# Moving the loads of two weight matrices and of half of x behind the first tile of y, and planning the modulation loads with later landings

## The chip, the core and the metric

One core of a Trainium2 chip. The metric is the device time of one execution in microseconds, lower is better. Times are read from a hardware profile of one execution and from repeated unprofiled executions of the same program.

## What is computed

All tensors are bf16. S = 2048 positions, D = 640 channels, F = 1728 hidden features.

```python
mod = silu(c) @ w_mod            # (640) @ (640, 6*640) -> sa, ca, ga, sb, cb, gb
h = layernorm(x) * (1 + ca) + sa
# A: a shift filter of 4 taps on k, times v, then a long causal convolution over S by FFT
kv = shift4(k, shift_k) * v
y  = irfft(rfft(kv, 4096) * rfft(ssm_k, 4096))[:S] + kv * ssm_D
x  = x + ga * (h * y)
h  = layernorm(x) * (1 + cb) + sb
# B: w1, gelu, shifts along S by +-1 and +-2 rows per quarter of the channels, w2; then w3, gelu, w4
h1 = h + shifts(gelu(layernorm(h) @ w1)) @ w2
out = x + gb * (h1 + gelu(layernorm(h1) @ w3) @ w4)
```

## The kernel before

The convolution is a two-level FFT made of matmuls. It works on channels in five blocks of 128 (`b`), then on positions in 16 tiles of 128 (`A` or `t`).

Stages, by their helper functions:

- `stage1` (L408) and `stage2` (L425): the forward transform of the filter s, block by block. `to_slots` (L395, a 32x32 transpose on DVE) brings each block into shape; `evac` (L208 on ACT, L210 on DVE) copies each PSUM result to SBUF.
- `k_shift` (L480, evacuated by a multiply with v, L485): the 4-tap shift. k and v come in transposed, one block at a time, by transposing DMAs on SP's queue (L234). Each multiplied block then goes through `to_slots`, `stage1` (L408) and `stage2_half` (L446).
- `inverse1` (L633 multiplies, L644 and L645 matmuls) and `inverse2` (L685): the inverse transform. `inverse2` leaves y for two or three tiles at a time in `Rb`, called `y_all`.
- `mod_half` (L503 load, L509 matmul, L516 to L524 evacuation): one half (320 columns) of one of the six modulation vectors. Twelve halves in the order ga, ca, sa (the first six; buffers in `RH` and `RK`, three in rotation) and then cb, sb, gb (the last six; buffers in `R3`).
- `x_load` (L540), `ln1_stats` and `ln1_fin` (L554 to L577), `make_q` (L610, L617, L618): the first layernorm and q.
- `chain_a`, `chain_b`, `chain_c`: for a tile, x += q*y with the sum for the next layernorm (L761, L764); a sum of squares on ACT (L753); the scale, made on POOL (L738 to L741); the second h (L775 or L779, then L780); its layernorm (L748 or L610). `turn` transposes the result by PE (L796) for the first tiles and by DMA on SP (L789) for the later ones.
- `mm_w1` (L842, L852), `mm_w2` (L897), `mm_w3` (L931), `mm_w4` (L961): the four matmul layers of B, in groups of one or two tiles. The result goes out from SP (L993).

Nothing is scheduled on the chip. Every piece of work is a task of the `Planner`, in a list with a number. A text, `ORDER`, gives the order in which all tasks are issued: a task number, a letter for its engine (P TensorE, A ScalarE, D VectorE, G GpSimd, S the SP queue), and, for matmuls, the PSUM buffers (0 to 3) that it uses. `run` only checks that a task's dependencies stand ahead of it in the list:

```python
            assert t.deps <= seen and len(places) == len(t.alloc)
```

The costs, the landing times (`lat`, `rate`) and the reads and writes (`r`, `w`) given to `add` served the search that produced the text. The waits on the chip come from the layer below, which finds which instructions touch the same memory. Each engine takes its own instructions in the order of the text.

In `ORDER` of before, SP has the last six modulation halves, one 40 KB piece of w2 among them, then x of tiles 8 to 15 in four transfers of 320 KB, mixed with w1 (800 KB), w2 (640 KB and four pieces of 40 KB) and the tail of w4. w3 and w4 take the place of what `inverse2` reads.

Of the kernel before, what the change touches and what calls it, by code (L numbers as in the profile page):

```python
# [15 lines left out]
S, D, F = 2048, 640, 1728  # L16
P = 128
# [9 lines left out]
18D 19G 20D 21G 23D 24A 22D 27G 29D 36G 37G 30A 28D 50G 0S 2S 68G 69D 25A 31A 26G 84P:0 86P:1 88P:2 51D 53A 4S 72G 73D 106P:3 85A 87A 38G 104P:0 89A  # L27
107A 6S 3S 70G 71D 39G 40A 102P:1 103A 5S 74G 98P:2 99A 105D 8S 90P:3 91A 49G 118P:0 75D 110P:1 9S 119D 94P:2 32G 111A 95A 112P:3 113A 108P:0 109A
116P:1 114P:2 115A 1S 66D 67D 96P:3 117D 80P:0 82P:1 10S 122P:2 41G 42G 43G 44A 97A 52D 54A 45D 81A 83D 11S 123D 33G 78P:3 79A 100P:1 101D 76P:0 77A
136D 92P:2 34S 47S 120P:3 121D 93A 179P:1 55G 180A 46S 7S 193P:0 194A 35S 195P:2 196A 181P:1 147P:0 148A 182D 201S 141P:3 142D 139P:2 140A 143P:1  # L30
199P:0 175P:3 200A 48S 176A 144D 204S 185P:2 186D 161P:1 162A 65G 157P:0 158D 171P:3 172A 203S 165P:2 166D 191P:1 192A 167P:0 155P:3 156A 168D 169P:2
170A 177P:1 178D 189P:0 190A 151P:3 159P:2 160A 202S 152D 145P:1 146D 187P:0 188A 149P:3 150D 197P:2 198A 183P:1 184D 153P:0 154A 163P:3 164A 262P:2
173P:1 174A 12S 137P:0 138A 13S 214D 263A 126P:3 56G 264P:1 210D 254D 127D 57G 124P:0 125D 211D 58G 59G 60A 61G 62G 63G 265A 260P:2 215A 266P:1 267A
261A 14S 255D 64A 15S 128P:3 129D 258P:0 259A 270P:1 271A 130P:2 131D 256D 16S 212A 276P:0 277A 268P:1 269A 132P:3 134P:2 17S 133D 135D 257D 282P:0
209A 283A 223S 213G 224P:1 225A 220S 278P:3 226S 286P:2 287D 279A 221P:0 222A 272P:1 273A 274P:3 275A 227P:0 228D 469D 284P:1 463D 342S 285A 292P:2
293D 288P:0 289A 232S 233P:3 234D 290P:1 291D 466D 296P:2 297A 294P:0 295A 229S 230P:3 231D 343G 310P:1 302P:2 303A 311D 235S 460D 312P:3 313A 298P:0
299D 308P:1 309A 236P:2 237D 467D 300P:3 301A 306P:0 307D 280P:2 281A 316P:1 317D 252G 314P:3 315A 253S 304P:0 305D 318P:2 319A 248G 247G 320P:1 321A
241S 336P:3 340P:2 341A 337A 243G 240S 330P:0 331A 338P:1 339A 367G 251S 250G 239S 326P:2 322P:3 323A 464D 345D 344D 348P:0 349A 244G 346P:1 347A 352D
245S 249G 334P:3 238S 242S 351G 246G 335A 350S 353D 356P:0 357A 354P:1 366S 324P:3 325A 327D 359G 332P:2 333A 358S 360D 361D 362P:0 363A 368D 364P:3
328P:2 329A 355A 369D 370P:0 371A 365A 376D 375G 374S 372P:2 377D 378P:1 379A 380P:0 373A 381A 384D 217A 382S 383G 385D 388P:3 389A 391G 390S 393D  # L40
392D 386P:1 400D 387A 396P:2 397A 394P:0 398S 399G 401D 402P:3 425S 403A 404P:1 405A 408D 395A 426P:2 407G 406S 409D 416D 410P:3 415G 414S 417D 412P:1
431S 411A 465D 413A 461D 462D 427D 216G 420P:0 421D 418P:3 419A 470D 422S 423P:1 424D 471D 468D 218A 475P:20 476A 477D 520D 499D 434S 456S 500D 521D
540D 541D 543D 459G 472A 435P:3 436A 523D 473D 474D 432P:1 437S 438P:2 219G 501A 433A 512A 478P:03 439A 522A 502G 503G 428S 429P:1 430A 504D 505D 542A
491P:21 525D 479A 524G 507D 526D 528D 492A 506A 480A 568D 527A 545D 485P:02 487A 493A 486A 206S 544G 546D 547A 207S 508G 509D 510P:3 529G 511A 530D
531P:2 532A 482P:10 481G 569D 570A 548D 452S 571D 572D 574D 573A 458G 517P:3 518A 205S 513D 536P:2 533D 484D 549G 483A 550D 534D 575G 580D 581D 576D
455S 582D 457S 577D 578D 208S 514D 538P:3 584D 537A 535D 634D 635D 631D 539A 583A 488P:01 551P:2 552A 579A 585G 586D 515P:3 589D 632D 449D 489A 558P:2
516A 637D 559A 556P:0 557A 636A 453S 587P:3 633A 638G 590P:2 591A 490A 497S 588D 454S 560P:0 561D 562A 643D 600P:2 601A 639D 494S 563G 564G 598P:3
599A 498G 640D 641D 565D 566P:1 602P:0 605P:2 642A 644D 645D 647D 646A 648G 441D 649D 650S 567A 618P:3 446A 616P:1 603D 604A 651D 652S 620P:0 553A
496S 619A 606D 661P:2 617A 443D 607A 440D 608G 609G 613D 659P:3 610D 622P:1 444D 621A 554D 555D 699D 700D 662A 660A 614P:0 615A 611P:2 666P:3 667D
663P:0 612A 683P:2 623A 442G 664D 701A 668A 684A 665A 669G 670G 671A 679P:1 680A 677P:3 495S 674D 672P:0 675P:2 678A 592D 593D 595D 596D 597D 673A  # L50
594D 702D 624P:1 676A 749P:3 765D 766D 703D 704A 681P:0 747P:2 750A 682A 445G 653D 654D 655D 768D 769D 770A 705G 706G 625D 626D 767A 745P:3 685P:10
748A 743P:2 771G 707D 708D 711D 709D 710A 686P 712D 713D 772G 773D 777A 715G 714A 716G 717A 718S 774D 778D 779D 780A 775D 776A 744A 781D 719D 720S
687D 746A 447D 782G 783A 785D 448G 729P:1 730A 786S 727P:2 728A 784S 795P:3 721A 656D 693D 796A 657D 658D 831D 628S 832D 793P:0 450D 694D 724A 451G
722D 734P:1 723D 794A 834D 835D 836A 697S 787D 735D 731P:2 732D 737D 797P:3 798D 833A 751P:01 696S 688D 837G 838G 843D 800P:2 736A 725D 752P 844D 845D
733A 738G 741D 689S 839A 840D 841D 739A 801D 803D 627S 799A 847D 802A 740S 842A 846A 742S 753D 811P:3 812A 804G 807D 805A 815P:2 788D 809P:0 848G 851D
816A 813P:3 810A 849D 726D 852S 850S 855P:2 856A 808S 790D 853P:0 806S 873P:2 759D 854A 860P:1 791D 792D 891D 892D 789D 951D 952D 954D 857P:0 894D
895D 629S 893A 814A 861D 897D 896A 630S 898G 899D 900D 858D 863D 692S 875P:3 876A 871P:1 869P:3 691S 872A 754D 757S 870A 695S 817P:01 901D 874A
877P:32 818P 862A 859A 864G 903D 819D 758S 904D 905D 906A 865D 867D 868S 866S 907D 902A 908G 909D 911D 953A 955G 956D 957D 935P:0 936A 958D 960G 959A
961G 878P 690S 760D 825D 756S 912S 755S 519G 962D 826D 885D 910S 915P:0 916A 913P:1 914A 698S 820D 879D 931P:0 762S 963S 966P:2 967A 964P:1 917P:3
918D 920P:2 921D 822S 965A 969P:1 970D 932A 968G 1003P:0 933P:3 929P:2 827S 828S 919A 922A 923G 924G 927D 928S 764S 925D 926S 1004D 1005A 972P:1 973D  # L60
934A 971A 930A 937P:03 987P:2 761S 988A 981P:1 983P:2 763S 880D 884S 883S 824S 823S 821S 886D 887S 890S 939D 975D 974A 976G 985P:0 977A 979D 889S 982A
829S 938P 945D 882S 984A 978S 986A 980S 1016P:1 1014P:2 1010P:0 1017A 1011A 881S 1015A 1012P:3 1006G 1007G 1008D 1009S 989P:10 1013A 946D 830S 940D
941S 991D 947S 1032P:2 888S 992D 993S 996S 943S 1038P:3 990P 997D 1036P:1 1033A 1042D 1037A 1018P:20 995S 949S 1034P:1 1035A 1019P 944S 942S 998D
1002S 1000S 999S 950S 1020D 948S 1021D 1023S 1025S 1026D 1039A 994S 1027D 1001S 1024S 1040P:21 1022S 1043D 1030S 1028S 1031S 1044D 1045D 1047S 1048S
1046S 1029S 1049S 1041P 1050D 1051D 1055A 1052S 1053A 1054S
# [72 lines left out]
def kernel(  # L138
# [63 lines left out]
    def dma(eng, kb, fn, r=(), w=(), rate=330.0):  # L202
        return add(eng, {"SP": 0.5, "POOL": 0.6}, lambda e: fn(nc.sync if e == "SP" else nc.gpsimd), r, w, kb=kb, rate=rate)
# [297 lines left out]
    def mod_half(i, j, hf):  # L501
        w, wk = wm[i % 3] if i < EARLY else wl[i - EARLY]
        dma("SP", 410, lambda q: q.dma_start(w, mod_d[:, :, j * D + 320 * hf:j * D + 320 * hf + 320]), w=[wk], rate=340.0)  # L503
# [34 lines left out]
    def x_load(a0, a1):  # L538
        for cg in range(4):
            dma("SP", 41 * (a1 - a0), lambda q, cg=cg: q.dma_start(x_all[32 * cg:32 * cg + 32, a0:a1, :], x_pos.rearrange("(a c) n d -> c n a d", c=4)[cg, :, a0:a1]),  # L540
                w=[("Ra", D * a0, D * a1, "x")], rate=275.0)
# [39 lines left out]
    x_load(8, NT)  # L581
# [77 lines left out]
    junk = RG[:, 7040:7680]  # L659
    ln1_all((8, 10), (10, 12), (12, 14), (14, 16))  # L660
    dma("SP", 800, lambda q: q.dma_start(w1_sb, B_w1.rearrange("(b p) n -> p b n", p=P)), w=[("RG", 0, 3200)])
    dma("SP", 700, lambda q: q.dma_start(w2_sb[:, 0:4, :], B_w2.rearrange("(g r) n -> r g n", g=4)[0:P]), w=[("RG", 3200, 6400, "w2")])
    for g in range(4):
        dma("SP", 60, lambda q, g=g: q.dma_start(w2_sb[32 * g:32 * g + 32, 4, :], B_w2[160 * g + P:160 * g + 160, :]), w=[("RG", 3200, 6400, "w2")])
    add("POOL", 0.8, lambda e: nc.gpsimd.tensor_copy(w1x.rearrange("p b (g r) -> p b g r", g=4), w1_sb.rearrange("p b (g r) -> p b g r", g=4)[:, :, :, P:160]),
# [423 lines left out]
```

## Time and profile before

| What | us |
| --- | --- |
| median of 3 runs | 303.29 (301.24 to 303.41) |
| the profiled execution, whole | 302.69 |
| its span in the profile | 301.0 |
| busy: PE, PEld, DVE, ACT, POOL | 271.0, 207.3, 220.8, 204.4, 108.9 |
| first matmul | 8.43 |
| first matmul of inverse2 | 98.20 |
| first y evacuated | 100.67 |
| PE at half clock (windows of 2 us that show 0.50) | 106 to 118, and 124 to 126 |
| PE without holes from | 143.13 |

The page's slices give, for each engine, the busy share of a fortieth of the span (7.5 us) in tenths; the windows give the same in us of 10. The chain is the work that ended last, followed back to what released each step; "issue" is time in which an engine waited for nothing that the profile shows. SP's rows are the issue of DMAs, not their transfer.

### The profile page before, as it was taken

How to read it: one execution, taken by the hardware profiler on the slowest of the kernel's cores; microseconds unless marked ns; L12 is line 12 of the kernel's file. 1: busy time of each engine (PE TensorE's matmuls, PEld its weight loads, DVE VectorE, ACT ScalarE, POOL GpSimd, SP SyncE). 2: the span in 40 equal slices, each digit the busy share in tenths (PEclk: the TensorE clock that was granted, in tenths of full speed). 3: DMA queues.
4: the chain of work that ended last, by engine and by line, in shares of the span. 5: the costliest groups of instructions: out<-in, count | busy, mean ns of one | idle time of the engine just before them, and what ended most of it. 6: DMA issues, size and time to landing. Idle time of an engine off the chain costs nothing.

```text
span 301.0 us, 7658 instructions
## 1 busy us (share of the span) xinstructions
PE 271.0 (90%) x3054; PEld 207.3 (69%) x3054; DVE 220.8 (73%) x446; ACT 204.4 (68%) x345; POOL 108.9 (36%) x238
## 2 busy tenths in 40 slices
PE   0899999979989576878999999999999999999993
PEld 0665655758888345756888787688867887887771
DVE  7999999979999979998659969983547343231343
ACT  4798999979999869998864679646451642604110
POOL 4967641451256646242345534310125120300000
PEclk9999999999999955799999999999999999999999
DMA  5998999998899940352900040234014112310121
GB/s 180 272 221 189 200 195 234 235 201 215 224 258 293 257 107 2 108 208 44 293 6 1 2 93 14 54 68 43 18 23 93 40 29 60 75 30 19 46 54 45
DMA packets 58179, 35.75 MB, mean 119 GB/s; under 512 B 39872, under 2 KB 54848, under 8 KB 58144
## 3 DMA queue, kind: packets, MB, share of 16 engines
q1 hardware_dynamic: 56944, 31.88, 45.2%
q0 software_dynamic: 1104, 3.34, 4.2%
q8 instruction: 24, 0.39, 0.5%
q14 instruction: 11, 0.09, 0.1%
q10 hardware_dynamic: 96, 0.04, 0.1%
HBM read 16.31 MB, written 2.62 MB: 63 GB/s over the span
## 4 chain that ended last, share of the span: by engine, by line
PE 71%; ACT 11%; DVE 6%; DMA 6%; issue 3%; POOL 1%; SPq 0%; ACTq 0%; DVEq 0%; POOLq 0%
PE ps_w L931 19%; PE ps_w L961 19%; PE ps_w L897 6%; PE ps_ksh L480 6%; PE ps_s L408 6%; PE ps_w L842 4%; ACT T L208 4%; ACT R L208 3%; PE ps_s L425 2%; PE ps_mod L509 2%; DMA RH<-in_w_mod_dram 2%; DMA Ra<-in_A_ssm_k_dram 2%; DVE R L780 1%; PE ps_i L644 1%; PE ps_s L446 1%
## 5 line engine op out<-in xcount | busy, mean ns | idle before, releaser
L931 PE MATMUL ps_w<-R,T 128*128 128x256 bf16 (+1 forms) x630 | 64.0, 261 | 0.0
L931 PEld LDWEIGHTS <-T 128*128 128x128 bf16 x630 | 55.7, 98 | 7.2 <-issue 1.1
L961 PE MATMUL ps_w<-T,R 128*128 128x320 bf16 x416 | 59.2, 299 | 0.0
L935 ACT ACTIVATE R<-ps_w 128x1024 bf16<-128x1024 f32 (+2 forms) x36 | 29.1, 828 | 42.1 <-PE ps_w L931 42.1
L961 PEld LDWEIGHTS <-R 128*128 128x128 bf16 x416 | 40.2, 98 | 15.8 <-ACT R L935 0.3
L208 ACT CAST T<-ps_s 128x1024 bf16<-128x1024 f32 x34 | 32.7, 1023 | 1.1 <-PE ps_s L408 1.1
L984 DVE TENSOR_TENSOR T<-ps_w,R 128x640 bf16<-128x640 f32 x15 | 12.3, 823 | 27.3 <-PE ps_w L961 14.0
L408 PE MATMUL ps_s<-F1bd,Rb 128*128 128x256 bf16 x160 | 22.9, 294 | 8.4 <-DVE Rb L395 8.4
L753 ACT ACTIVATE RG<-R 128x640 bf16<-128x640 bf16 x32 | 23.6, 736 | 10.2 <-DVE R L904 7.1
L208 ACT CAST R<-ps_s 128x640 bf16<-128x640 f32 (+1 forms) x36 | 26.7, 828 | 2.8 <-PE ps_s L446 1.9
L738 POOL TENSOR_TENSOR lnv<-stat,lnv 128x2 f32<-128x2 f32 x19 | 4.9, 256 | 62.6 <-ACT RG L753 33.0
L408 PEld LDWEIGHTS <-Rb 128*128 128x128 bf16 x160 | 16.4, 105 | 14.7 <-DVE Rb L395 8.8
L904 DVE SCALAR_TENSOR_TENSOR R<-ps_w,R 128x640 bf16<-128x640 f32 x16 | 13.1, 821 | 14.5 <-PE ps_w L897 14.5
L739 POOL TENSOR_TENSOR lnv<-lnv,mhalf 128x2 f32<-128x2 f32 (+1 forms) x29 | 22.3, 770 | 2.3
L897 PE MATMUL ps_w<-RG,R 128*128 128x320 bf16 x160 | 23.1, 299 | 0.0
L842 PE MATMUL ps_w<-R,RG 128*128 128x256 bf16 (+1 forms) x200 | 21.0, 267 | 0.3 <-ACT Rb L208 0.3
L644 PE MATMUL ps_i<-EA,Rb 128*128 128x128 bf16 x160 | 19.1, 219 | 1.2 <-ACT T L208 0.4
L645 PE MATMUL ps_i<-EB,Rb 128*128 128x128 bf16 x160 | 19.0, 219 | 0.5 <-DVE Rb L633 0.5
L897 PEld LDWEIGHTS <-R 128*128 128x128 bf16 x160 | 15.4, 98 | 6.0 <-issue 0.3
L842 PEld LDWEIGHTS <-RG 128*128 128x128 bf16 x200 | 18.2, 107 | 1.7 <-issue 0.4
L480 PE MATMUL ps_ksh<-R,RQ 128*128 128x512 bf16 x80 | 18.8, 380 | 0.0
L858 ACT ACTIVATE R<-ps_w1x 32x256 bf16<-32x256 f32 (+1 forms) x40 | 13.2, 330 | 7.8 <-PE ps_w1x L852 7.5
(179 smaller groups left out, 524.3 us busy)
## 6 DMA issues: line engine op xcount, KB each, us to landing
Ra<-in_A_ssm_k_dram SPq DMA_DIRECT2D x5, 512.0 KB, 5.6
Ra<-in_A_q_dram SPq DMA_DIRECT2D x8, 320.0 KB, 6.7
R<-in_w_mod_dram SPq DMA_DIRECT2D x6, 400.0 KB, 6.3
out_dram<-RH SPq DMA_DIRECT2D x60, 40.0 KB, 1.6
T<-in_B_w_dram SPq DMA_DIRECT2D x1, 2160.0 KB, 8.5
T<-in_B_w_dram SPq DMA_DIRECT2D x1, 2080.0 KB, 9.5
RH<-in_w_mod_dram SPq DMA_DIRECT2D x4, 400.0 KB, 4.3
RK<-R POOLq DMA_DIRECT2D x5, 256.0 KB, 4.5
```

The costliest lines, as they stand in the source:

```text
L208: nc.scalar.copy(dst, src(ps.tile))
L408: nc.tensor.matmul(psv[:, ml, :], lhsT=xL[:, s0:s0 + P], rhs=F1r, start=True, stop=True)
L480: nc.tensor.matmul(pt[:, i, :], lhsT=diagw[:, b, jj, :], rhs=kT[:, b, c0:c0 + 512], start=(jj == 0), stop=(jj == 3))
L644: nc.tensor.matmul(psv[:, w, :], lhsT=Av[:, r_, :, g_], rhs=EAf, start=True, stop=False)
L645: nc.tensor.matmul(psv[:, w, :], lhsT=Bv[:, r_, :, g_], rhs=EBf, start=False, stop=True)
L739: nc.gpsimd.tensor_tensor(rs, rs, mhalf[:, 0:n], ALU.pow)
L753: add("ACT", 0.74, lambda e: nc.scalar.activation(junk, src, ACT.Square, scale=float(D) ** -0.5, accum_out=stat[:, li, 1, t:t + 1]), r=[sk ...
L842: nc.tensor.matmul(pt[:, fb, 0:cw], lhsT=w1_sb[:, b, 160 * fb:160 * fb + P], rhs=hT[:, b, 0:cw], start=(b == 0), stop=(b == ND - 1))
L897: nc.tensor.matmul(pt[:, hf, 0:320], lhsT=gsf[:, fb, c0:c0 + P], rhs=w2_sb[:, fb, 320 * hf:320 * hf + 320], start=(fb == 0), stop=(fb == 4))
L931: nc.tensor.matmul(pt[:, fl, 0:cw], lhsT=w3_sb[:, b, fb * P:(fb + 1) * P], rhs=xT[:, b, 0:cw], start=(b == 0), stop=(b == ND - 1))
L935: nc.scalar.activation(g3[g % 2][:, f0:f0 + fn, 0:cw], ps.tile[:, 0:fn, 0:cw], ACT.Gelu_apprx_tanh)
L961: nc.tensor.matmul(bank(i, hf), lhsT=gg[:, fb, i * P:(i + 1) * P], rhs=w4_sb[:, fb, 320 * hf:320 * hf + 320], start=(fb == 0 and i == 0), ...
```

## The change

- The tasks of w1, w2, the copy of a part of w1 (`w1x`), x of tiles 8 to 15 and their statistics move down in the program, to behind the first call of `inverse2`, and the loads get a read of the first tile of y, `("Rb", 0, D)`, in their list of dependencies.
- x of tiles 8 to 15 comes in eight transfers of 160 KB instead of four of 320 KB.
- The modulation loads get `lat=1.5`, a landing 1.5 us later in the plan.
- The text `ORDER` is another one throughout. Tasks behind the moved ones have other numbers.

```diff
 ORDER = """
-18D 19G 20D 21G 23D 24A 22D 27G 29D 36G 37G 30A 28D 50G 0S 2S 68G 69D 25A 31A 26G 84P:0 86P:1 88P:2 51D 53A 4S 72G 73D 106P:3 85A 87A 38G 104P:0 89A
...
+18D 19G 20D 50G 21G 23D 22D 25A 27G 29D 30A 36G 37G 24A 28D 31A 2S 0S 68G 4S 26G 69D 90P:0 91A 6S 84P:1 85A 3S 72G 86P:2 87A 5S 32D 73D 102P:3 38G
...
-    def dma(eng, kb, fn, r=(), w=(), rate=330.0):
-        return add(eng, {"SP": 0.5, "POOL": 0.6}, lambda e: fn(nc.sync if e == "SP" else nc.gpsimd), r, w, kb=kb, rate=rate)
+    def dma(eng, kb, fn, r=(), w=(), rate=330.0, lat=0.0):
+        return add(eng, {"SP": 0.5, "POOL": 0.6}, lambda e: fn(nc.sync if e == "SP" else nc.gpsimd), r, w, kb=kb, rate=rate, lat=lat)
...
-        dma("SP", 410, lambda q: q.dma_start(w, mod_d[:, :, j * D + 320 * hf:j * D + 320 * hf + 320]), w=[wk], rate=340.0)
+        dma("SP", 410, lambda q: q.dma_start(w, mod_d[:, :, j * D + 320 * hf:j * D + 320 * hf + 320]), w=[wk], rate=340.0, lat=1.5)
...
-    def x_load(a0, a1):
+    def x_load(a0, a1, r=()):
         for cg in range(4):
             dma("SP", 41 * (a1 - a0), ...
-                w=[("Ra", D * a0, D * a1, "x")], rate=275.0)
+                r=r, w=[("Ra", D * a0, D * a1, "x")], rate=275.0)
...
     x_load(0, 8)
-    x_load(8, NT)
...
-    ln1_all((8, 10), (10, 12), (12, 14), (14, 16))
-    dma("SP", 800, lambda q: q.dma_start(w1_sb, ...), w=[("RG", 0, 3200)])
-    dma("SP", 700, lambda q: q.dma_start(w2_sb[:, 0:4, :], ...), w=[("RG", 3200, 6400, "w2")])
-    for g in range(4):
-        dma("SP", 60, lambda q, g=g: ..., w=[("RG", 3200, 6400, "w2")])
-    add("POOL", 0.8, lambda e: nc.gpsimd.tensor_copy(w1x ...
...
     inverse2([0, 1, 2])
+    y0 = [("Rb", 0, D)]
+    dma("SP", 800, lambda q: q.dma_start(w1_sb, ...), r=y0, w=[("RG", 0, 3200)])
+    dma("SP", 700, lambda q: q.dma_start(w2_sb[:, 0:4, :], ...), r=y0, w=[("RG", 3200, 6400, "w2")])
+    for g in range(4):
+        dma("SP", 60, lambda q, g=g: ..., r=y0, w=[("RG", 3200, 6400, "w2")])
+    add("POOL", 0.8, lambda e: nc.gpsimd.tensor_copy(w1x ...
+    x_load(8, 12, y0)
+    x_load(12, NT, y0)
+    ln1_all((8, 10), (10, 12), (12, 14), (14, 16))
     inverse2([3, 4])
```

What the new text does on the queues, as far as the prediction speaks of it:

| Queue | before | after |
| --- | --- | --- |
| SP, head | ssm_D, s block 1, s block 3 | s block 1, ssm_D, s block 3 |
| SP, transposes | four x loads, then k2 v2 k3 v3 k4 v4, then modulation halves | one x load, k2 k3, three x loads, v2, one modulation half, v3 k4 v4, further halves |
| copies of the FFT table (L354) | three on SP, one on POOL | one on SP, three on POOL |
| SP, late modulation | cb1, (inverse1 copies), sb1, cb0, gb0, a w2 piece, gb1, sb0, then x, x, w1, x, w2 pieces, x, w2 | cb1, (inverse1 copy), cb0, sb1, sb0, gb0, gb1, then w2, w1, eight x with the w2 pieces among them |
| PE, from inverse2 on | tiles 0-2, gb0, sb1, gb1, tiles 3-4, sb0, tiles 14-15, 8-10 | tiles 0-2, sb1, sb0, gb0, tiles 8-10, gb1, tiles 3-4, 14-15, 5-7 |
| ACT, sums of squares of chain_a | tile 1 ahead of sb0's evacuation, tile 2 behind it | tiles 1 and 2 behind gb1's evacuation |

(cb1 is the second half of cb, and so on.)

## The prediction

> **What bounds the kernel now.** I read the slices first, then the windows, then the chain that ended last, then PE's and SP's timelines where the chain leaves PE.
>
> ```profile
> PE   0899999979989576878999999999999999999993
> DVE  7999999979999979998659969983547343231343
> ACT  4798999979999869998864679646451642604110
> PEclk9999999999999955799999999999999999999999
> DMA  5998999998899940352900040234014112310121
> ```
>
> ```profile
> 90.00:100.00 10.00, 9.28 (x212) 7.89 (x210) 9.96 (x15) 9.65 (x14) 5.69 (x9) 1.00 1.04 277
> 100.00:110.00 10.00, 5.93 (x145) 3.02 (x143) 7.94 (x20) 6.47 (x15) 6.02 (x13) 0.79 0.92 222
> 110.00:120.00 10.00, 7.20 (x227) 5.67 (x227) 9.62 (x26) 9.65 (x19) 6.75 (x20) 0.53 0.01 3
> 150.00:160.00 10.00, 10.00 (x92) 8.10 (x90) 6.72 (x17) 6.01 (x11) 4.02 (x11) 1.00 0.03 11
> ```
>
> The columns of the second view are PE, PEld, DVE, ACT, POOL busy, clock, DMA share, GB/s. There are two kernels in one. Up to about 143 us ACT and DVE are nearly full and PE waits for them; from 143 us on PE is full to the end (10.00 of 10) and the others have room. The end is the moment at which PE fills up, plus a fixed amount of matmul work. So the change is worth what it moves that moment, less any hole it makes in PE afterwards.
>
> The chain leaves PE in two places that the change touches:
>
> ```profile
> 55.59 6.57 DMA RH<-in_w_mod_dram
> 62.20 0.85 PE ps_mod L509 x5
> ...
> 98.20 1.20 PE ps_i L685 x88
> ...
> 102.09 3.70 issue
> 105.79 0.97 PE ps_i L685 x41
> 106.76 1.46 PE ps_mod L509 x5
> 108.24 0.43 ACT modv L524
> 108.77 0.90 DVE R L780 x2
> ```
>
> At 62 us PE waits for modulation weights (1.55 us idle; DVE then loses 1.65 and ACT 1.85 us). At 102 us PE stands for 3.70 us with nothing to wait for. PE's timeline shows why:
>
> ```profile
> 98.20 1.20 PE L685 MATMUL ps_i<-T,RH 32*32 32x160 bf16 x96 [0.42 <-ACT T L208]
> 99.33 2.21 PE L509 MATMUL ps_mod<-R,silu_w 128*128 128x320 bf16 x15
> 101.47 0.62 PE L685 MATMUL ps_i<-T,RH 32*32 32x160 bf16 x22
> 105.79 0.97 PE L685 MATMUL ps_i<-T,RH 32*32 32x160 bf16 x42 [3.70 <-issue]
> ```
>
> 96+15+22 matmuls, each with its weight load, are 266 instructions since 98.20: about one block of instructions. Inverse2 uses them up in 4 us, while the DMA engines are full (share 0.92 over 100 to 110 us), and the next block is late. One half of the shift weights, whose matmuls are behind the hole, then holds ACT for 2.67 us and DVE for 1.74.
>
> **The Trainium skill.** "Runtime: NRT & Kernel Launch", Instruction fetch mechanics: instructions come in blocks of 16 KiB, 256 instructions, on a DMA queue of the sequencer, and crossing a block is mostly hidden. The page's q8 agrees on size (24 packets, 0.39 MB); it is not hidden at 102 us. "DMA: Bandwidth & Descriptors", Issuing engines are not separate DMA queues: transfers from all engines share the same 16 DMA engines; the trace agrees, the block is late exactly under the loads. "TensorE: Matmul & The Clock Gate", Part 1: an idle window of about 3.4 us halves the clock; here it is 0.50 from 106 to 118 us, after 3.70 us idle.
>
> **The change part by part.**
>
> *1. The held loads.* The added reads of `Rb` are entries in the planner's own table, which asserts only that a task stands later in the list. On the built program the first moved load (w2) waits for an earlier DMA and for PE's last read of RG (stage 2), not for y. So nothing is held; the loads stand behind all six late modulation loads on SP and go out when these have. Where they stood before:
>
> ```profile
> 86.97 3.33 SPq L503 DMA_DIRECT2D R<-in_w_mod_dram x3
> 92.81 0.34 SPq L664 DMA_DIRECT2D RG<-in_B_w_dram x1
> 93.25 0.96 SPq L503 DMA_DIRECT2D R<-in_w_mod_dram x2
> 94.26 1.02 SPq L540 DMA_DIRECT2D Ra<-in_A_q_dram x2
> ```
>
> Only one 40 KB piece, which waits 2.4 us for DVE, was ahead of the last two modulation loads. Gain for those: about 2.4 us of landing. I expect w2 out near 92 us, 8 us before the first y is evacuated (100.67). The bytes are the same: 2.4 MB of modulation weights, 1.6 of w1 and w2, 1.3 of x. So the DMA engines stay full until about 109 us, and the late block stays. Four more x issues cost SP 4 x 0.5 us with nothing behind them until the w3 load, which waits for inverse2 until 122 us: nothing. The last small piece of w2, that landed at 125.68 behind the w4 tail, comes earlier; its first reader starts at 128.95: nothing.
>
> *2. Early modulation halves.* In the new order the first modulation load stands on SP between the transposes of v for blocks 2 and 3, and its matmuls free its buffer before the last transpose, so the fourth load no longer waits for PE (54.04). The 1.55 us hole at 62 goes: DVE -1.6.
>
> *3. The price on SP.* The transposes set the pace from 38 to 55 us: v of block 4 lands at 50.41, its multiply (L485) runs at 51.69.
>
> ```profile
> 26.85 1.71 SPq L540 DMA_DIRECT2D Ra<-in_A_q_dram x3
> 28.59 6.09 SPq L234 DMA_TRANSPOSE R<-in_A_k_dram x1
> 34.73 2.43 SPq L234 DMA_TRANSPOSE R<-in_A_v_dram x1
> 37.21 3.09 SPq L234 DMA_TRANSPOSE R<-in_A_k_dram x1
> ```
>
> A transpose takes 2.5 us, but 6.09 behind 1.28 MB of loads: it waits until they are through. Now two transposes come before three of the x loads, two after, and 400 KB before the last three. Estimate from these rows: start 26.0 (two copies moved from SP to POOL), k2 to 29.5, k3 to 32.2, x to 33.9, v2 to 40.3 (3.9 for the x, 2.5 its own), load and v3 to 44.9, k4 47.4, v4 49.9, landed 52.2 (2.3 after its issue, as 48.05 to 50.41 before), 1.8 later. DVE would come to v2 at 41.5 and gets it at 42.6 (waits 1.1); the new order puts other work before the later blocks, which wins 0.2 back. So block 4's DVE transpose ends about 0.9 later than the 56.16 of before. DVE +0.9.
>
> *4. Order and engines up to the first inverse2.* The first block of s is issued before the tiny load: -0.5 (1.32 to 0.79). DVE gets one L349 (0.28), one L461 (0.15) and one stage-2 evacuation (0.78) more, ACT one (0.63) less: +0.6 in sum, half of it on the path, +0.3. A further swap, one inverse1 evacuation to DVE for one stage-1 evacuation to ACT, is even. Sum of 2 to 4: -1.6 +0.9 -0.5 +0.3 = -0.9. Bounds -2.5 and +4.
>
> *5. From inverse2 to a full PE.* The matmuls of the shift's two halves now come directly behind the first inverse2, ahead of the hole; behind it comes a half of gb, which nobody needs yet. But its evacuation stands on ACT ahead of the sums of squares of tiles 1 and 2. With the block usable 7.6 us after inverse2 begins (98.2 to 105.79): rest of [8,9,10] 1.25, modulation 1.46 (both at half clock), ACT 0.42+0.93+0.93, POOL 1.2: tile 2's scale is ready 7.6+1.25+1.46+2.3+1.2 = 13.8 us after inverse2's start, and the three h tiles are done at about 16.1; before, 114.2-98.2 = 16.0. Tile 0 gains 2 us, tiles 1 and 2 lose it: 0. DVE's list up to the first pair that is transposed by DMA has 4 PSUM copies (1.6), one statistic (1.1), one half finish (0.5) and one multiply (0.4) more, two finishes (0.9), two norms (0.8), a w2 sum (0.8) and a y evacuation (1.1) less: 0. I take 0; bounds -3.7 and +2.
>
> *6. The full stretch.* The same matmuls. The transposed pairs arrive just in time: landed 176.38 for a matmul at 177.30. Every group's order is new, so +0.4, bounds 0 and +2.
>
> Sum: -0.9 + 0 + 0.4 = -0.5 on the profiled execution's 302.69 (span 301.0, 1.7 around it): 302.2. The median of the three runs is 0.6 above that execution; I say **302.4**.
>
> **Rivals.** *A, faster:* the late block comes in time, since at 98 us the outstanding loads are smaller (160 KB of x each) or the loads are held after all. Then the half clock goes too, tiles 1 and 2 are not held, and the 3.7 us are won: 298.7. For it: at 89 us, also under full DMA, the block came in time. Against it: the same bytes are in the way.
> *B, slower:* the transposes. If each of the three that stand behind a load takes 6.1 as k2 did, then from 26.0: k2 32.1, k3 34.8, x 36.5, v2 42.6, load 43.1, v3 49.2, k4 51.7, v4 54.2, landed 56.6, 4.4 past my 52.2. DVE and ACT have no room there, so all of it lasts: 306.8. It decides from a landing of v4 past about 56 us. Against it: 6.09 was behind four loads.
> *C, a hole in PE after 143:* a late pair costs what it is late, four pairs by 1 us each 4 us more, 306.4. Against it: DVE is at 40 to 67% there.
> *D, nothing:* 2 and 3 cancel and the rest is noise: 303.3.
>
> **How the numbers follow.** A measurement of this kernel tells about 1% (3 us) from no change. Forecast 0.40, D 0.10, A 0.23, B 0.19, C 0.08. Faster by over 1%: A, 0.23; slower: B and C, 0.27; within: 0.50. The range reaches from just under A to just over B: 297.5 to 307.5; the forecast alone would be 300.5 to 305.
>
> **What would show it.** Right: w2 issued before 95 us and before y; no wait of L509 for DMA at 62; the late block again near the second inverse2, clock 0.5 after it; PE full from about 143; v4 landing near 52. Wrong: SP waiting for ACT or DVE ahead of w2; no 3 us of "issue" (A); DVE waiting for k_shift's v tiles for over 3 us in all (B); PE idle after 150 (C).

## The result: 4.5% slower, and the profile after

| | before | after |
| --- | --- | --- |
| median | 303.25 us (301.24 to 303.41, 4 runs) | 315.75 us (314.98 to 318.61, 4 runs) |
| span of the profiled execution | 301.0 | 313.0 |
| first matmul of inverse2 | 98.20 | 105.27 |
| PE full from | 143.13 | 149.89 |
| last matmul ends | 296.22 | 308.04 |

The ratio is 1.0445, 95% interval 1.0378 to 1.0513: 12.5 us slower, outside the predicted range. All ratios here leave out a run that is over 1.5% above the fastest of its kernel. The table splits the 12.0 us of span. 7.07 are lost before inverse2 starts, 0.3 is won from there to a full PE (44.62 against 44.93), 5.06 are lost after PE is full (158.15 against 153.09), and the rest, 0.2, is at the end. The split is a fair one: behind the moment at which PE is full, both kernels have the same 1,318 matmuls to do. So there are two losses, in different stages. The page's slices of after show both:

```profile
PE   0998999999973846687999978989999999999993
DVE  8998999999964999989776586881627144511332
ACT  4888999999991789998974666625763445252110
PEclk9999999999995965999999999999999999999998
DMA  6998999988999910521800031043021403131021
```

In the thirteenth slice (94 to 102 us) PE shows 3, DVE 4 and ACT 1. Behind the twentieth, where before showed only nines, PE has a 7 and two 8 (slices 24, 25 and 27: 180 to 211 us). The windows give it in us (columns as before):

```profile
90.00:100.00 10.00, 3.61 (x47) 3.21 (x48) 3.42 (x4) 4.31 (x6) 2.11 (x5) 0.76 1.13 273
100.00:110.00 10.00, 8.54 (x202) 7.05 (x204) 9.23 (x15) 6.30 (x11) 4.03 (x9) 0.90 0.93 235
110.00:120.00 10.00, 5.05 (x255) 2.85 (x256) 9.68 (x28) 9.00 (x18) 8.32 (x22) 0.61 0.07 21
150.00:160.00 10.00, 10.00 (x96) 8.40 (x95) 7.94 (x25) 8.04 (x19) 1.54 (x3) 1.00 0.67 222
180.00:190.00 10.00, 7.27 (x60) 5.47 (x58) 8.83 (x23) 6.72 (x12) 1.99 (x4) 1.00 0.37 74
200.00:210.00 10.00, 8.98 (x73) 6.87 (x71) 8.46 (x21) 3.30 (x7) 2.65 (x8) 1.00 0.38 78
```

From 90 to 100 us PE, DVE and ACT all work for about 4 us of 10 while the DMA engines are full (1.13): everyone waits for a transfer. DVE's timeline names it, and POOL's timeline says why it is late. First DVE of after (start, duration, what, and in brackets the idle time with what ended it):

```profile
88.88 2.35 DVE L632 TENSOR_TENSOR Rb<-R,R 128x2048 bf16<-128x2048 bf16 x2
97.81 1.22 DVE L632 TENSOR_TENSOR Rb<-R,RG 128x2048 bf16<-128x2048 bf16 x1 [6.58 <-DMA RG<-R]
```

POOL of after, and below it POOL of before in the same stage:

```profile
80.94 0.51 POOL L628 DMA_DIRECT2D Rb<-R  x1 [1.76 <-DVE Rb L632]
81.47 1.50 POOL L572 TENSOR_TENSOR nb<-mv 128x1 f32<-128x1 f32 x1
83.05 0.19 POOL L573 TENSOR_TENSOR mv<-mv,nb 128x1 f32<-128x1 f32 x1
83.19 1.28 POOL L572 TENSOR_TENSOR nb<-mv 128x1 f32<-128x1 f32 x1
84.55 1.05 POOL L573 TENSOR_TENSOR mv<-mv,nb 128x1 f32<-128x1 f32 x1
...
89.10 1.09 POOL L577 TENSOR_SCALAR nb<-nb 128x2 f32<-128x2 f32 x1
90.12 0.62 POOL L628 DMA_DIRECT2D RG<-R  x1
90.75 0.53 POOL L628 DMA_DIRECT2D RK<-R  x1
...
106.95 0.19 POOL L573 TENSOR_TENSOR mv<-mv,nb 128x1 f32<-128x1 f32 x1 [0.72 <-ACT RQ L563]
...
108.99 0.35 POOL L577 TENSOR_SCALAR nb<-nb 128x2 f32<-128x2 f32 x1
```

```profile
81.31 0.51 POOL L629 DMA_DIRECT2D Rb<-R  x1 [1.76 <-DVE Rb L633]
83.58 0.51 POOL L629 DMA_DIRECT2D RG<-R  x1 [1.76 <-DVE Rb L633]
86.26 0.51 POOL L629 DMA_DIRECT2D RK<-R  x1 [2.17 <-DVE Rb L633]
86.78 0.37 POOL L572 TENSOR_TENSOR nb<-mv 128x1 f32<-128x1 f32 x1
```

The rows with DMA_DIRECT2D are POOL's halves of the `inverse1` copies of the spectrum (the other halves go out on SP). In before the last three go out at 81.31, 83.58 and 86.26, and only then comes `ln1_fin` of tiles 4 and 5 (L572 to L577). In after `ln1_fin` stands ahead of the last two. Its eight small operations take from 81.47 to 90.12, and the copies that were ready at about 83 and 84.5 us (SP issued its halves at 82.95 and 84.44) go out at 90.12 and 90.75. The first lands at 97.62, DVE gets on at 97.81 after 6.58 us, and inverse2 follows 7.07 us late. Nobody needs this `ln1_fin` soon: the first norm that reads it stands behind inverse2 in the list.

The second loss is in PE's timeline of after:

```profile
185.88 0.71 PE L843 MATMUL ps_w1x<-R,RG 128*128 128x256 bf16 x5 [1.75 <-DMA R<-RK]
...
189.75 2.34 PE L833 MATMUL ps_w<-R,RG 128*128 128x256 bf16 x20 [0.98 <-DMA R<-RK]
```

```profile
206.64 5.62 PE L922 MATMUL ps_w<-R,T 128*128 128x256 bf16 x50 [1.02 <-DVE RK L609]
...
277.12 7.80 PE L922 MATMUL ps_w<-R,T 128*128 128x256 bf16 x70 [0.52 <-DMA R<-RH]
```

Four times PE waits for a pair of tiles that is transposed by DMA: twice in `mm_w1` for the pairs of tiles 7, 8 and 9, 10, and twice in `mm_w3` for tiles 6, 7 and 14, 15. That is 4.27 us of idle time where before had none; counted from start to start of the matmuls on both sides, the four holes cost 4.9 of the 5.06 us. (For the third the profile names DVE, whose L609 had written something else; the second transpose of the pair, issued at 203.91, lands at 206.51.) For the first, POOL and ACT again show the chain:

```profile
166.57 0.20 POOL L572 TENSOR_TENSOR nb<-mv 128x1 f32<-128x1 f32 x1
...
172.20 0.80 POOL L577 TENSOR_SCALAR nb<-nb 128x2 f32<-128x2 f32 x1
172.97 0.75 POOL L729 TENSOR_TENSOR lnv<-stat,lnv 128x2 f32<-128x2 f32 x1
```

```profile
174.81 0.92 ACT L607 ACTIVATE R<-Ra,lnv 128x640 bf16<-128x640 bf16 x1 [1.54 <-POOL lnv L732]
```

Two more `ln1_fin` (tiles 12 to 15) hold POOL from 166.57 to 172.97, ahead of the `ln_finish` (L729) of tiles 9 and 10, whose sum of squares ended at 171.4. ACT stands 1.54 us at the norm that needs it, and the sums of squares of tiles 7 and 8 stand behind that norm.

### The profile page after: what moved, and what is told of

Same layout as the page of the kernel before. It is cut to its first block, busy times and chain, and to the rows that moved or that the text cites. A ratio compares the mean times of both kernels' runs of the same rounds, so it can differ in the third digit from the quotient of the medians.

```text
span 313.0 us, 7669 instructions
## 1 busy us (share of the span) xinstructions
PE 270.4 (86%) x3050; PEld 206.3 (66%) x3054; DVE 219.6 (70%) x446; ACT 208.5 (67%) x351; POOL 114.2 (36%) x240
## 4 chain that ended last, share of the span: by engine, by line
PE 41%; DVE 12%; ACT 6%; DMA 5%; POOL 4%; issue 3%; SPq 0%; ACTq 0%; DVEq 0%; POOLq 0%
PE ps_w L952 15%; PE ps_w L922 14%; PE ps_w L888 5%; PE ps_w L833 3%; ACT RG L744 3%; DMA RG<-R 2%; DVE R L771 2%; DMA R<-RH 1%; DVE Ra L755 1%; POOL lnv L730 1%; PE ps_w1x L843 1%; PE ps_w L943 1%; DVE R L770 1%; PE ps_i L644 1%; DMA R<-RK 1%
## 5 line engine op out<-in xcount | busy, mean ns | idle before, releaser
L408 PEld LDWEIGHTS <-Rb 128*128 128x128 bf16 x160 | 16.5, 105 | 15.4 <-DVE Rb L395 8.8
L644 PE MATMUL ps_i<-EB,Rb 128*128 128x128 bf16 x160 | 20.3, 227 | 6.7 <-DVE Rb L632 6.7
L730 POOL TENSOR_TENSOR lnv<-lnv,mhalf 128x2 f32<-128x2 f32 (+1 forms) x29 | 23.1, 796 | 2.3
L208 ACT CAST T<-ps_i 128x1024 bf16<-128x1024 f32 x18 | 17.6, 1126 | 8.9 <-PE ps_i L644 8.9
L729 POOL TENSOR_TENSOR lnv<-stat,lnv 128x2 f32<-128x2 f32 x19 | 5.8, 306 | 46.0 <-ACT RG L744 31.6
L833 PE MATMUL ps_w<-R,RG 128*128 128x256 bf16 (+1 forms) x200 | 19.0, 251 | 3.2 <-ACT Rb L208 1.4
L643 PE MATMUL ps_i<-EA,Rb 128*128 128x128 bf16 x160 | 20.5, 227 | 1.4 <-DVE Rb L632 1.1
L644 PEld LDWEIGHTS <-Rb 128*128 128x128 bf16 x160 | 16.3, 103 | 7.4 <-DVE Rb L632 7.4
L833 PEld LDWEIGHTS <-RG 128*128 128x128 bf16 x200 | 16.4, 98 | 5.1 <-issue 2.4
```

Source lines behind the costliest of these rows:

```text
L208: nc.scalar.copy(dst, src(ps.tile))
L408: nc.tensor.matmul(psv[:, ml, :], lhsT=xL[:, s0:s0 + P], rhs=F1r, start=True, stop=True)
L643: nc.tensor.matmul(psv[:, w, :], lhsT=Av[:, r_, :, g_], rhs=EAf, start=True, stop=False)
L644: nc.tensor.matmul(psv[:, w, :], lhsT=Bv[:, r_, :, g_], rhs=EBf, start=False, stop=True)
L730: nc.gpsimd.tensor_tensor(rs, rs, mhalf[:, 0:n], ALU.pow)
L833: nc.tensor.matmul(pt[:, fb, 0:cw], lhsT=w1_sb[:, b, 160 * fb:160 * fb + P], rhs=hT[:, b, 0:cw], start=(b == 0), stop=(b == ND - 1))
```

## The experiments

Kernel 1 is the kernel of experiment 1, and so on. All entries are those of after's `ORDER` unless before is named. Each time is a median; each ratio is to before, measured beside it on the same chip, with its 95% interval.

**1. `ln1_fin` of tiles 4 and 5 behind the copies.**

```diff
-... 392P:3 390P:1 212G 394S 397D 396D 213A 400P:0 402S 391A 404D 403G ... 411G 413D ...
+... 392P:3 390P:1 394S 397D 396D 213A 400P:0 402S 391A 404D 403G ... 411G 212G 413D ...
```

> After, with one entry of ORDER moved: ln1_fin of tiles 4 and 5 (212G) stands on POOL behind the last two inverse1 copies (403G, 411G), as in before, not ahead of them. Theory P (POOL's queue): those copies were issued at 90.12 and 90.75 only because the eight small POOL operations stood ahead of them; they now go out beside their SP halves, at about 83 and 84.5 us, land by 92, DVE's 6.58 us wait in L632 goes, the first y is evacuated near 100.8 and not 108, and the kernel loses about 7 of its 12.5 us: 308.5 us, 1.017 times before. If the late block of instructions then comes back at the second inverse2 (3.7 us in before, about 1 in after), up to 311. Theory L (the transfers): the copies are late since modulation halves, w2, w1 and x fill the 16 DMA engines; then they still land past 95 us and the time stays at 314 or more.

310.21 us, ratio 1.0213 (1.0160 to 1.0267). The copies go out at 83.91 and 85.22 and land at 89.54 and 92.26; DVE does not wait in L632 and inverse2 starts at 98.21. One entry of a list of 1,060 is worth 5.5 of the 12.5 us by the medians (315.75 to 310.21), 6.0 when each is set against the before measured beside it. It is less than the 7.07 because the late block of instructions is back:

```profile
98.21 1.20 PE L676 MATMUL ps_i<-T,RH 32*32 32x160 bf16 x96 [0.42 <-ACT T L208]
99.34 2.21 PE L509 MATMUL ps_mod<-R,silu_w 128*128 128x320 bf16 x15
101.48 0.37 PE L676 MATMUL ps_i<-T,RH 32*32 32x160 bf16 x22
105.19 1.43 PE L676 MATMUL ps_i<-T,RH 32*32 32x160 bf16 x74 [3.33 <-issue]
```

96+15+22 matmuls and then 3.33 us of issue, as before had it (3.70). In after the same hole was 1.04 us (109.95), since inverse2 came when the loads were nearly through.

**2. The same entry the other way, in before.**

```diff
-... 407G 406S 409D ... 415G ... 427D 216G 420P:0 ...
+... 216G 407G 406S 409D ... 415G ... 427D 420P:0 ...
```

> Before, with one entry of ORDER moved: ln1_fin of tiles 4 and 5 (216G) stands on POOL ahead of the last two inverse1 copies (407G, 415G), as in after. Theory P: the two copies go out at about 89.5 and 90 instead of 83.58 and 86.26, land near 96, DVE waits 4 to 6 us in L633, and the time becomes about 308.5 us, 1.017 times before. Theory L: nothing else is moved, so the copies land at most 1 us later than 91.5 and the time stays within 1% of before.

Ratio 1.0073 (1.0040 to 1.0105), about 2.2 us. Its 20 runs spread from 303.3 to 309.8 us, and the median of all is 307.55, 3.8 above before's 303.72. That is less than the 308.5 expected, and the ratio alone lies within the 1% that theory L allows. The profiled execution (307.17) decides between the two:

```profile
81.32 0.37 POOL L572 TENSOR_TENSOR nb<-mv 128x1 f32<-128x1 f32 x1
...
87.52 0.62 POOL L629 DMA_DIRECT2D RG<-R  x1
88.14 0.52 POOL L629 DMA_DIRECT2D RK<-R  x1
```

The copies go out at 87.52 and 88.14 and land at 95.10 and 96.00, where theory L had at most 92.5. DVE stands 4.29 us in L633 and goes on at 95.18, right after the first landing (the profile calls this wait issue). Theory P holds in both directions. Its size is smaller here, 4.7 us at the first matmul of inverse2 (102.88 against 98.20): before's `ln1_fin` has six of these operations, not eight, and takes 6.20 us, not 8.65.

**3 and 4. Loads that are really held, without and with the first edit.** A DMA of a few columns of the first y stands ahead of w2 on SP:

```diff
+    def w2_behind_y(q):
+        q.dma_start(RG[:, 7808:7824], y_all[:, 0, 0:16])
+        return q.dma_start(w2_sb[:, 0:4, :], B_w2.rearrange("(g r) n -> r g n", g=4)[0:P])
+
-    dma("SP", 700, lambda q: q.dma_start(w2_sb[:, 0:4, :], ...), r=y0, ...)
+    dma("SP", 700, w2_behind_y, r=y0, ...)
```

> After, with the loads really held: the w2 task first issues a DMA of 16 columns of the first y tile to an unused place, so that SP's queue stands until y is there. w2, w1 and x go out at about 108 and not from 92.12 on. Theory P: the late copies are still issued at 90.12 and 90.75, and land perhaps 1 us sooner; inverse2 starts at about 104.5; w1, w2 and the late x are now 15 us later and may hold the first mm_w1: 313 to 318 us. Theory L: with w2, w1 and x out of their way the copies land by 94, and the first y comes at 104 or sooner: 311 us.

317.29 us, ratio 1.0456 (1.0395 to 1.0517). w2 is issued at 109.20, not at 92.12, and still the copies go out at 90.06 and 90.68 and land at 97.79 and 99.71, as in after (97.62, 99.75). So w2, w1 and x were not what made them late: theory L falls for these. The modulation loads, its other part, were not varied; but in kernel 1 they are as they were, and the copies land in time once POOL issues them. What is left for the transfers is small: the first late copy takes 7.50 us in after and 7.73 here, against 5.63 in kernel 1.

> Both edits: ln1_fin of tiles 4 and 5 behind the copies, and the loads really held behind the first y. Theory P: first y near 100.5 and w2 out just behind it. If the late block of instructions comes from full DMA engines, as the prediction says, there is no hole of 3 us of issue near the second inverse2 and this is faster than the kernel with the moved ln1_fin alone by what hole is left there (1 to 3.7 us), if w1 at about 112 us comes in time for the first mm_w1: 305 to 308 us. If w1 and x come too late: slower than it, by up to 4 us. Theory L: as the first kernel, both gains add, 308.

308.14 us, ratio 1.0141 (1.0104 to 1.0178). The 3.33 us of issue are gone, PE's next block is there at 101.94 without a hole, and PE is full from 143.40 (145.20 in kernel 1). By the medians that is 2.1 us for the hole, not 3.3.

The trace has the block itself. PE's instructions come in the packets of queue q8 that the prediction counted. The packet behind inverse2's first 133 matmuls moved from 102.89 to 104.19 us in before and from 102.35 to 103.71 in kernel 1, and PE went on at 105.79 and 105.19. In kernel 4 it moved from 99.27 to 100.25, before PE came to its end of the block. The next two packets of kernel 4 (from 104.50 and from 111.69) fall among the loads that were let go at 101.67, and there PE stands for 0.52 and 0.81 us with nothing to wait for.

**5. The other two `ln1_fin` earlier on POOL**, added to kernel 4:

```diff
-... 754A 481G 774A 775D 478G 750A ... 776G ...
+... 480A 478G 481G 618P:3 ... 754A 774A 775D 750A ... 776G ...
```

> The kernel with ln1_fin of tiles 4 and 5 behind the copies and the loads really held, and on POOL also ln1_fin of tiles 12-13 and 14-15 (478G, 481G) moved from directly ahead of ln_finish of tiles 9-10 (776G) to behind the last statistic that they need (480A), where POOL stands idle for 7 us. Theory Q (POOL's queue again): the two ln1_fins, 6.4 us of small operations, hold 776G by about 1.6 us, ACT stands at the norm that waits for it with two sums of squares behind, and the transposes of tiles 7 to 10 are late; the first hole of PE after it has filled (1.6 us at mm_w1 of tiles 7 and 8) goes and the second (0.9) shrinks: 306 us. Theory R: the pairs are late for DVE's and ACT's own order, or for the transposes' 2.6 us: the holes stay within 0.4 us and the time at 308.

307.23 us, ratio 1.0105 (1.0064 to 1.0145). The first hole goes from 1.69 to 0.22 us, the second only from 1.0 to 0.83, the third stays (0.98). The two ratios overlap, so the gain of 0.9 us rests on the trace. Theory Q is right for the first hole; the second shrank by only 0.17, and of the third it said nothing. The 306 us that it expected were not reached.

**6. Really held loads in before.** The first late load of x gets the same DMA of y ahead of it, and the early w2 piece (456S) goes behind it.

> Before, with the loads behind inverse2 really held: the first load of x of tiles 8 to 15 is preceded by a DMA of 16 columns of the first y tile, and the one w2 piece that stood among the modulation halves goes behind it. Nothing else is moved. The late block of instructions should then be there in time, no 3.70 us of issue at 102. The prediction's rival A put that hole at its full 3.7 us: 299.6. Theory S: DVE lost only 1.74 us by it and ACT 2.67, and these two are the bound up to 143 us, so 1 to 2 us are won: 301.5. If the late x and w1 hold something up: 303 or more.

301.51 us, ratio 0.9928 (0.9897 to 0.9958): faster than both kernels. PE's timeline where before had 3.70 us of issue:

```profile
101.72 1.03 PE L689 MATMUL ps_i<-T,RH 32*32 32x160 bf16 x64
104.00 0.84 PE L509 MATMUL ps_mod<-R,silu_w 128*128 128x320 bf16 x5 [1.25 <-ACT modv L524]
105.14 0.49 PE L689 MATMUL ps_i<-T,RH 32*32 32x160 bf16 x16 [0.29 <-ACT modv L524]
106.18 1.01 PE L689 MATMUL ps_i<-T,RH 32*32 32x160 bf16 x48 [0.55 <-ACT modv L524]
```

The issue is gone here, but PE now waits for ACT (1.25, 0.29, 0.55). ACT and DVE are the bound in this stage, and they had lost 2.67 and 1.74 us by the hole, not 3.70. That is theory S: the hole is worth about what these two lose, 1.7 us by the medians. The half clock did not go with it: windows of 2 us show 0.50 from 106 to 118 us in kernel 6 as in before, though PE's longest idle stretch between inverse2's start and 106 us is now 1.25 us and not 3.70.

**7 and 8. The early modulation load alone in before, and with held loads.**

```diff
-... 12S 137P:0 138A 13S 214D ... 283A 223S 213G 224P:1 ...
+... 12S 137P:0 138A 13S 223S 214D ... 283A 213G 224P:1 ...
```

> Before, with one load moved on SP: the first modulation half (223S) stands between the transposes of v of block 2 and k of block 3, as the change has it. By steps 2 and 3 of the prediction: PE's hole of 1.55 us at 62 (waiting for modulation weights) goes or halves, the later transposes come about 1 to 2 us later, net -1 to +1: 301.7 to 303.7. If a transpose behind a load costs 6 us each: 306.

304.44 us, ratio 1.0030 (1.0009 to 1.0052). The hole did not close, it grew:

```profile
62.73 0.85 PE L509 MATMUL ps_mod<-RH,silu_w 128*128 128x320 bf16 x5 [2.21 <-DMA RH<-in_w_mod_dram]
```

The load is issued at 36.00 and lands at 41.08, but PE reads it at 53.03, where its matmul stands in PE's order (53.17 in before). So its buffer comes free no sooner and the fourth load goes out at 53.90 (before 54.04). The load that PE waits for at 62 is the fifth, right behind it: out at 55.46, it takes 7.22 us (before 6.57 from 55.59). The earlier load alone is not what closed the hole in after: there the first of these matmuls stands sooner in PE's order too (49.08), the fourth load is out at 51.66, and the fifth, out at 57.31, takes 4.61 us.

> Before with both edits of the two kernels above. If they act in different stages and each only on its own: the sum of the two differences, about 301 us. If the second only shifts where DVE waits: as the held loads alone.

301.47 us, ratio 0.9894 (0.9841 to 0.9948): as the held loads alone, within the intervals.

**9 and 10. The halves of the two orders exchanged**, both with held loads and with `ln1_fin` of tiles 4 and 5 behind the copies. Kernel 9 has after's order up to the first evacuated y and before's from there on, kernel 10 the reverse.

> Two halves of ORDER put together: up to the first evacuated y the order of after (with ln1_fin of tiles 4 and 5 behind the copies), from there on the order of before, with the loads really held and x in eight transfers. To be read against before with held loads (301.5). Theory V: what is left of the loss when POOL's queue and the late block are taken out (about 4 us) lies wholly in the order behind inverse2; up to there the two orders are equal (the second block of inverse2's instructions began at 98.5 in both): 300.5 to 302.5, PE full near 141.6 and without holes. Rival: the order up to inverse2 leaves something behind (DVE or ACT work not yet done, evacuations put off): 304 or more.

> The other way round: the order of before up to the first evacuated y, from there on the order of after, loads really held. To be read against after with held loads and ln1_fin of tiles 4 and 5 behind the copies (308.1). Theory V: the same 307 to 309, PE full near 143.5, then holes of together 3 to 4 us from 175 to 200, for the order behind inverse2 brings them. Rival: 304 or less.

301.39 us, ratio 0.9934 (0.9913 to 0.9956), and 308.49 us, ratio 1.0155 (1.0100 to 1.0211). Theory V holds in the times: the order up to inverse2 is worth nothing either way, apart from POOL's entry; the order behind it costs 7 us. Kernel 9's profiled execution (303.07) is among the slowest of its 22 runs: its inverse2 starts at 99.36, and PE is full from 143.57 and not from 141.6 as expected, but then without holes. The windows of kernel 9, then of kernel 10:

```profile
170.00:180.00 10.00, 10.00 (x85) 7.69 (x83) 6.68 (x18) 6.59 (x12) 4.67 (x12) 1.00 0.35 69
180.00:190.00 10.00, 10.00 (x82) 7.67 (x80) 9.66 (x28) 9.17 (x17) 4.83 (x12) 1.00 0.05 13
190.00:200.00 10.00, 10.00 (x83) 7.59 (x82) 8.15 (x24) 5.74 (x11) 2.83 (x8) 1.00 0.23 49
```

```profile
170.00:180.00 10.00, 8.62 (x70) 6.19 (x69) 8.16 (x21) 6.57 (x12) 3.69 (x6) 1.00 0.19 39
180.00:190.00 10.00, 8.89 (x75) 7.05 (x73) 7.21 (x18) 6.83 (x14) 1.28 (x5) 1.00 0.22 46
190.00:200.00 10.00, 9.11 (x69) 6.03 (x67) 8.13 (x21) 5.48 (x13) 4.12 (x11) 1.00 0.21 43
```

PE is full in one and stands for 3.4 us in the other. Kernel 10's span of 306.6 is 6.8 longer than kernel 6's: 1.9 until PE is full (143.65 against 141.75, inverse2 at 98.46 and 98.44), about 3.8 of holes after that, 1.1 elsewhere. In the stretch of the 1.9 work was pulled ahead: from inverse2 to a full PE, ACT has three norms more (2.7 us), one layernorm statistic of two passes more (1.9) and one evacuation more (1.0), against five copies of transposed tiles fewer (3.5), which DVE does now (2.4). In sum ACT is busy for 1.3 us more and DVE for 2.1. That this work is the 1.9 was not tested.

**11. Two entries on SP**, added to kernel 5:

```diff
-... 790S 795D 661D 787D 788S 797P:1 ... 745D 702S 746S ...
+... 795D 661D 787D 788S 790S 797P:1 ... 745D 746S 702S ...
```

> The kernel with held loads and all three ln1_fins in better places, and on SP two entries moved: the transpose of tile 9 (788S) ahead of that of tile 10 (790S), which waits longer for ACT, and an output store (702S, 0.57 us) from between the two transposes of the pair of tiles 6 and 7 (744S, 746S) to behind them. Theory: these two holes of PE, 0.83 us at the second mm_w1 and 0.98 at mm_w3, last as long as the second transpose of the pair is late; each should become 0.5 to 0.6 us shorter, the rest of the kernel as it was: 306 us, against 307.2. Rival: the holes are ACT's and POOL's lateness, and only move: 307.

305.81 us, ratio 1.0080 (1.0051 to 1.0109). With the output store out of its way the second transpose of the `mm_w3` pair goes out at 194.83, right behind the first (195.45 before), and the hole shrinks from 0.98 to 0.40. The other swap changed nothing (the two go out at 177.33 and 178.62, as before at 177.31 and 178.61); that pair landed at 181.22 in both, and its hole went from 0.83 to 0.56 because PE came 0.3 us later. From a full PE to the last matmul this kernel needs 155.0 us, kernel 5 156.9, before 153.1.

## Why the prediction was wrong, point by point

- *Step 1, the loads are not held*: right. w2 was issued at 92.12 (I had said near 92), 14.6 us before the evacuation of the first y began (106.72). That the late block stays was right for an inverse2 at 98 us (kernel 1) and wrong for after, where inverse2 came later. That the loads make the block late is shown by kernels 4 and 6: with the loads held the hole is gone, and the packet moves about 3 us sooner (from 99.27 and 99.80).
- *Step 2, the hole at 62*: it went in after, and DVE's wait of 1.65 us with it, but the -1.6 us did not reach inverse2: kernel 1 starts it at 98.21, before at 98.20. Which other term took them was not taken apart. Kernel 7 shows that the early load alone does not close the hole; in after the first of the matmuls also stands sooner in PE's order. The step also named the fourth load for the hole; it is the fifth that PE waits for.
- *Step 3, v of block 4 landing at 52.2*: it landed at 52.96, 0.8 later. Rival B (past 56) did not come.
- *Step 4, the order up to the first inverse2*: **this step failed.** Steps 2 to 4 were to sum to -0.9 with bounds of -2.5 and +4; it was +7.07. The step counted what DVE, ACT and PE get and lose and left POOL's list out, where one `ln1_fin` had moved past two copies. Without that entry the sum was 0.0. Before's own rows had the price: six of the same operations from 86.78 to 92.84.
- *Step 5, inverse2 to a full PE at 0*: -0.3 in after, but +2.06 with inverse2 in its old place and the hole of issue there (46.99 in kernel 1 against 44.93), just past its bound of +2. The small number in after is luck: inverse2 came late enough to miss most of the hole. The count of DVE's list was right in kind; ACT's norms and statistics that came ahead were missed.
- *Step 6, the full stretch at +0.4, bounds 0 and +2*: **failed too**: +5.06. The prediction's rival C, a hole in PE after 143 by late pairs, is what happened, and at its size: it had four pairs and 4 us, the four holes have 4.27. It had a chance of 0.08 because DVE had room there. Room on DVE does not help a pair that waits for POOL or SP, each in its own order.
- *Rival A* had the mechanism right and the price wrong: the hole of 3.70 us is worth 1.7 (kernel 6) to 2.1 (kernel 4), near what ACT and DVE lose by it. It also had the half clock go with the hole, since the prediction puts the half clock down to those 3.70 us of idle PE. In kernel 6 the clock falls all the same, with no idle stretch over 1.25 us: here the measurement does not bear out the idle window that the prediction names for it. What the fall takes was not tested.
- *The sum*: 302.2 for the profiled execution and 0.6 from there to the median make 302.8, not the 302.4 that was said. Nothing hangs on it.

Of the 12.5 us, 5.5 to 6 are thus one entry on POOL; it hid 2.1 more that the late block costs. Kernels 5 and 11 won back 2.3 of the second loss. Kernel 11 is still 4.4 us above kernel 9, which has before's order behind inverse2: that much lies in this order (in the profiled executions 1.3 us from inverse2 to a full PE and 1.8 after it), and which entries it is was not taken apart.

## What to carry to other kernels

Where a whole order is replaced, list for every engine, also for the one with the lowest busy share, what has moved past each DMA that it issues: POOL was at 36% and cost the most. A hole in PE in a stage where other engines set the pace is worth about what these lose by it, not its own length. A dependency that only a planner sees holds nothing on the chip; a small DMA of the data in question ahead of the loads does.

## What the runs showed of the hardware

- Small POOL operations took more than twice as long while DVE ran its long two-operand multiplies back to back. The Trainium skill, "SBUF — State Buffer", section "SBUF: two separate sides", says that a DVE operation with two SBUF inputs and a POOL operation that reads SBUF take a shared port in turn, each for a whole instruction; "Perfetto Trace Analysis", GPSIMD Engine Instruction, says to time POOL by the spacing of starts. So read, the last five operations of `ln1_fin` (L573 to L577) took 5.57 us in after beside the multiplies (84.55 to 90.12) and 2.39 at 107 us (106.95 to the end at 109.34). That agrees with the lock but does not show it: no run here took the multiplies away.
- For a late block of instructions PE stood at inverse2 for 3.70 us (before), 3.33 (kernel 1) and 2.99 (kernel 2) under full DMA engines, for 1.04 in after when they were nearly done, and not at all when the loads behind it waited (kernels 4 and 6). The loads that were let go then met the next blocks: 0.52 and 0.81 us in kernel 4, 1.82 and 1.01 in kernel 11.
- Clock of PE: at 0.50 from 106 to 118 us with a hole of 3.70 us ahead of it (before) and without that hole (kernel 6).
